# 128 rows of the last head's output weights on three DMA engines, placed between the V groups of the load stream

## The chip, the cores and the metric

One core of a Trainium2 chip runs one step of attention with a KV cache, an MLP that gates it, and a residual. The metric is device time in microseconds (us) of one execution. "Fast" and "slow" are the labels that the measurement gives: slow is a run more than 1.5% above the fastest of the same kernel.

## The reference, cut to what matters

```python
xn = layernorm(x)                                   # x: 4 x 1 x 512
q  = (xn @ wq).reshape(4, 1, 32, 128)               # wq: 512 x 4096
o  = softmax(q @ k.T * 128**-0.5) @ v               # the last 1024 keys; 8 KV heads of 4 query heads
s  = o.reshape(4, 1, 4096) @ wo                     # wo: 4096 x 512
g  = silu(gelu(layernorm(xn) @ w1 + b1) @ w2 + b2)  # w1: 512 x 1792
return x + s * g
```

Everything is bf16, the batch is 4: 29 MB are loaded and each byte is used once.

## The kernel before: the parts that matter

The program gives every engine its own list of operations with the waits that they need. SyncE issues the large loads in one order: wq and K groups, then V groups with w1 and w2 among them, then the output weights wo. A V group takes the SBUF space of a K group. A load whose space is not free makes SyncE wait, and what stands behind it waits too: in this kernel's trace SyncE waits 21.7 + 8.7 us for TensorE, and issues no later load meanwhile.

```python
load_v(0); d_w1 = dma("sp", w1 ...); load_v(1); d_w2 = dma("sp", w2 ...)
for g in range(2, HKV):
    load_v(g)
wo_r = A_wo.rearrange("(g p i) o -> p g i o", g=HKV, i=4)   # 4 rows of each head on each partition
for n, (g0, g1, i0, i1) in enumerate(((0,2,0,4), (2,4,0,4), (4,6,0,4), (6,7,0,4),
                                      (7,8,0,3), (7,8,3,4))):
    d_wo.append(dma("sp", wo_sb[:, g0:g1, i0:i1, :] <- wo_r[:, g0:g1, i0:i1, :]))
# TensorE, from "S" on: scores, PV(0), first MLP product mlp1 (w1), PV(1), second MLP product (w2), PV(2..7)
rows = to_rows(0, HKV)          # 16 products: o of all heads to the rows that wo's partitions hold
for k in range(len(d_wo)):      # 128 products in six groups, each waits for its load
    t_w = wo(k, rows)
# then: times g, transpose, plus x, store
```

The softmax here doesn't subtract the row's maximum and nothing guards it: scores larger than these inputs give would overflow.

## Time and profile before

| kernel before | |
|---|---|
| time | 76.9 to 77.1 us in the first four runs, median 77.03 |
| span of the profiled execution | 75.3 us |
| loaded | 28.85 MB, some 428 GB/s from 52.5 to 57 us |
| third wo load landed on its last engine | 69.86 us |
| last wo load landed, first and last engine | 70.42 and 72.17 us |
| first MLP product ends | 51.70 us |

"Landed" is taken from the semaphore updates in the trace: a load to 128 partitions has 16 of them, read here as one per DMA engine (the page counts 16 engines). Two lines of TensorE's timeline show how little slack its end has (columns: start, duration, engine, source line, operation, how many; in brackets its idle time before and what ended it):

```profile
68.00 1.55 PE L507 MATMUL psM<-OW,wo_sb 128*128 128x4 bf16 x53 [0.51 <-DVE OW L493]
70.13 2.35 PE L507 MATMUL psM<-OW,wo_sb 128*128 128x4 bf16 x75 [0.58 <-issue]
```

The 128 wo products run without a visible wait but for one stop of 0.58 us that no semaphore explains. It comes 764 of TensorE's matmuls and weight loads after the last such stop before it; the earlier ones, which end at 27.95, 34.43, 40.45 and 46.84 us, are 254 apart. Inside the second line TensorE waited only 0.2 us for the fifth load.

### The profile page before, as it was taken

Reading aid. Unit: us, or ns where it says so; the run is one execution under the profiler, and the core shown is the slowest. Engines: PE = TensorE matmul, PEld = TensorE weight load, DVE = VectorE, ACT = ScalarE, POOL = GpSimd, SP = SyncE. Lnnn points to the kernel's source line nnn. Section 1 sums busy time; section 2 is a strip of 40 time slices with the busy share of each in tenths; the row PEclk is TensorE's granted clock in tenths of the full one; section 3 lists DMA queues with packets and bytes.
Section 4 is the critical chain, followed back from the end, with each engine's and each line's share of the span. In section 5 each row is a group of like instructions: output and inputs, shape, how many; then the busy total and the mean of one; then the engine's idle time right before and its main releaser. Section 6 shows DMA issues by size and latency. Waiting matters only on the chain.

```text
span 75.3 us, 2297 instructions
## 1 busy us (share of the span) xinstructions
PE 50.0 (66%) x1046; PEld 39.8 (53%) x1058; DVE 39.3 (52%) x82; ACT 9.8 (13%) x16; POOL 4.6 (6%) x14
## 2 busy tenths in 40 slices
PE   0000039993859949987997994999069879818770
PEld 0000039992359939976997860104049576518740
DVE  0778107786058967985996424001664679770010
ACT  0611000000090303111130630003300000000000
POOL 6980000000000000000000000000000000000000
PEclk9999999999999999999999999569755555555555
DMA  1899999998999999999999999999999999999600
GB/s 36 244 455 405 420 422 479 435 444 370 427 422 431 422 418 431 427 414 466 401 420 453 406 443 390 427 431 409 427 427 440 418 401 416 418 420 416 252 25 2
DMA packets 4219, 28.99 MB, mean 385 GB/s; under 512 B 493, under 2 KB 625, under 8 KB 1650
## 3 DMA queue, kind: packets, MB, share of 16 engines
q1 hardware_dynamic: 4160, 28.84, 92.2%
q8 instruction: 8, 0.13, 0.6%
q10 hardware_dynamic: 50, 0.01, 0.1%
q14 instruction: 1, 0.01, 0.0%
HBM read 28.85 MB, written 0.00 MB: 383 GB/s over the span
## 4 chain that ended last, share of the span: by engine, by line
DMA 36%; PE 35%; SPq 16%; issue 5%; DVE 4%
DMA wo_sb<-in_A_wo_dram 24%; PE psK L278 22%; SPq L475 15%; DMA kv_buf<-in_A_k_cache_dram 12%; PE psS L297 7%; PE psO L362 3%; DVE kt_buf L284 2%; DVE q_sb L368 1%; PE psK L374 1%; PE psM L507 1%; PE psK L346 1%; PE psS L538 1%; SPq L212 1%; SPq L205 0%; DVE o_bf L540 0%
## 5 line engine op out<-in xcount | busy, mean ns | idle before, releaser
L278 PE MATMUL psK<-ident,kv_buf 128*128 128x128 bf16 x256 | 21.2, 237 | 11.8 <-DMA kv_buf<-in_A_k_cache_dram 10.6
L284 DVE COPY kt_buf<-psK 128x1024 bf16<-128x1024 bf16 x32 | 21.3, 691 | 8.7 <-PE psK L278 8.6
L278 PEld LDWEIGHTS psK<-ident,kv_buf 128*128 128x128 bf16 x256 | 17.1, 108 | 11.1 <-DMA kv_buf<-in_A_k_cache_dram 10.6
L297 PE MATMUL psS<-qT,kt_buf 128*128 128x16 bf16 x256 | 10.4, 169 | 1.7 <-issue 1.1
L297 PEld LDWEIGHTS psS<-qT,kt_buf 128*128 128x128 bf16 x256 | 9.4, 96 | 3.0 <-issue 2.1
L315 PEld LDWEIGHTS psO<-P_buf,kv_buf 128*128 128x128 bf16 x256 | 7.4, 102 | 3.0 <-issue 3.0
L315 PE MATMUL psO<-P_buf,kv_buf 128*128 128x16 bf16 x256 | 8.0, 173 | 1.0 <-DVE OTb L333 0.6
L328 DVE TENSOR_REDUCE den_sb<-psS 128x16 f32<-128x512 f32 x8 | 5.5, 691 | 4.2 <-PE psO L315 4.0
L305 ACT ACTIVATE P_buf<-psS 128x512 bf16<-128x512 f32 x8 | 4.8, 597 | 17.1 <-PE psS L297 17.1
L400 PE MATMUL psK<-w_sb,yT 128*32 128x512 bf16 x16 | 4.9, 1093 | 1.3 <-issue 1.3
L507 PE MATMUL psM<-OW,wo_sb 128*128 128x4 bf16 x128 | 3.9, 166 | 1.1 <-issue 0.6
L507 PEld LDWEIGHTS psM<-OW,wo_sb 128*128 128x128 bf16 x128 | 3.6, 104 | 1.4 <-issue 1.2
L411 DVE SCALAR_TENSOR_TENSOR kt_buf<-kt_buf,psK 128x512 f32<-128x512 f32 x1 | 0.7, 686 | 6.4 <-ACT kt_buf L410 6.4
L534 DVE TENSOR_TENSOR sg_sb<-psM,g_sb 128x16 f32<-128x16 f32 x1 | 0.2, 185 | 4.7 <-PE psM L507 4.7
L400 PEld LDWEIGHTS psK<-w_sb,yT 128*32 128x32 bf16 x16 | 0.5, 114 | 3.8 <-issue 3.8
L369 ACT ACTIVATE q_sb<-psO 128x512 bf16<-128x512 f32 x1 | 0.6, 597 | 13.5 <-PE psO L362 13.5
L424 PE MATMUL psK<-ident,kt_buf 128*128 128x128 bf16 x4 | 0.6, 307 | 2.4 <-DVE kt_buf L419 2.4
L331 DVE RECIPROCAL rden<-den_sb 128x16 f32<-128x16 f32 x8 | 2.0, 253 | 0.3
L362 PE MATMUL psO<-wq_sb,xT 128*32 128x512 bf16 x32 | 1.9, 380 | 0.3 <-DVE xT L351 0.3
L246 DVE CAST P_buf<-x_bf 4x512 f32<-4x512 bf16 x1 | 0.8, 795 | 2.4 <-DMA x_bf<-in_A_x_dram 2.4
L237 POOL TENSOR_SCALAR_AFFINE_SELECT negm<-zero_bf 128x512 bf16<-128x512 bf16 x1 | 1.9, 1852 | 0.1
L321 PE MATMUL psS<-P_buf,ones_bf 128*128 128x512 bf16 x3 | 1.8, 587 | 0.0
(64 smaller groups left out, 27.4 us busy)
## 6 DMA issues: line engine op xcount, KB each, us to landing
kv_buf<-in_A_k_cache_dram SPq DMA_DIRECT2D x8, 1024.0 KB, 19.9
kv_buf<-in_A_v_cache_dram SPq DMA_DIRECT2D x8, 1024.0 KB, 22.8
wq_sb<-in_A_wq_dram SPq DMA_DIRECT2D x2, 2048.0 KB, 11.3
w_sb<-in_B_w_dram SPq DMA_DIRECT2D x2, 1792.0 KB, 27.9
wo_sb<-in_A_wo_dram SPq DMA_DIRECT2D x3, 1024.0 KB, 24.3
wo_sb<-in_A_wo_dram SPq DMA_DIRECT2D x1, 512.0 KB, 21.5
wo_sb<-in_A_wo_dram SPq DMA_DIRECT2D x1, 384.0 KB, 18.2
wo_sb<-in_A_wo_dram SPq DMA_DIRECT2D x1, 128.0 KB, 18.0
```

Of the source, the lines that this page charges most:

```text
L237: c_neg = add("gp", lambda e: e.affine_select(negm[:, :], zero_bf[:, :], [[0, 32], [1, 4], [0, 4]], ALU.is_equal, NEG, base=0, channel_mul ...
L278: last = pe.transpose(psK[n % NB][:, j * 128:(j + 1) * 128], kv_buf[:, g, u * UT + j, :], ident[:, :])
L284: cp[n] = add("dve", lambda e: e.tensor_copy(kt_buf[:, n % NKT, :], psK[n % NB][:, 0:1024]), t, sc.get(n - NKT))
L297: last = pe.matmul(psS[g % 2][:, c * 16:(c + 1) * 16], kt_buf[:, n % NKT, j * 128:(j + 1) * 128], qT[:, g * 16:(g + 1) * 16], start=False, ...
L305: ex[g] = add("act", lambda e: e.activation(P_buf[:, g, :], psS[g % 2][:, 0:512], AF.Exp, scale=SCALE), sc[n])
L315: last = pe.matmul(pso[:, 0:16], kv_buf[:, (HKV + g) % NS, c, :], P_buf[:, g, c * 16:(c + 1) * 16], start=(c == 0), stop=(c == NC - 1))
L328: v = add("dve", lambda e: e.tensor_reduce(den_sb[:, cs], bass.AP(psS[g % 2], 0, [[512, 128], [1, 16], [16, NC]]), AX.X, ALU.add), den[g])
L331: v = add("dve", lambda e: e.reciprocal(rden[:, cs], den_sb[:, cs]), v)
L362: last = pe.matmul(psO[m // 4][32 * s:32 * s + 32, 0:512], xT[:, c, :], wq_sb[:, c, m * 512:(m + 1) * 512], start=(c == 0), stop=(c == 3), ...
L400: pe.matmul(psK[0][32 * s:32 * s + 32, 0:1024].bitcast(F32), yT[:, c, :], bass.AP(w1_sb, c * F + K0[s], [[4 * F, 128], [1, 4], [FC, 128]]) ...
L475: e.dma_start(wo_sb[:, g0:g1, i0:i1, :], wo_r[:, g0:g1, i0:i1, :]))))
L507: last = pe.matmul(psM[:, PS_W + c * 4:PS_W + (c + 1) * 4], wo_sb[:, g, i, c * 128:(c + 1) * 128], OW[:, i, g * 4:(g + 1) * 4], start=firs ...
```

## The change

The intent: some DMA engines finish 1.4 us before the others (the prediction says why), so give the early ones more to do and the late ones less. The last 128 rows of wo go to a space of 24 partitions, 120 of them by a load whose shape is to confine it to three engines, and stand among the V groups. The space is that of w1, so the load waits until the first MLP product has read w1.

```diff
+    wox_sb = w1_sb[0:24, ...]                       # 24 partitions x 6 rows, over w1
+    sel3, selx, OW3, OWx ...                        # selectors for the new places of the rows; 3 GpSimd selects
-        t = add("pe", fn, v_xyT, d_w1, ...)
+        t = mlp["w1"] = add("pe", fn, v_xyT, d_w1, ...)
-    for g in range(2, HKV):
-        load_v(g)
     for g in range(HKV):
+        if g >= 2:
+            load_v(g)
+        if g == 4:
+            d_wox = [dma("sp", wox_sb[:, 0:5] <- [[5*D, 3], [15*D, 8], [1, 5*D]], mlp["w1"]),  # 120 rows
+                     dma("sp", wox_sb[0:8, 5] <- [[D, 8], [1, D]], mlp["w1"])]                 # 8 rows
         PV(g)
...
-    (7, 8, 0, 3), (7, 8, 3, 4)                      # last head: 3 + 1 rows a partition
+    (p i) o, i = 3: (0, 2), (2, 3)                  # last head's first 384 rows: 2 + 1 rows a partition
-    to_rows: 16 products; wo: 128 products
+    to_rows: 16 + 9 + 6 products; wo: 112 + 24 + 12; the 24 follow the third wo load's
```

More of the change, by code (lines that the diff above doesn't have):

```diff
@@ L124, in bass_recurrent_scan__sliding_block_cached__mixer_channel_mlp__decode_kernel @@
     w2_sb = sb([128, FC, D], BF16)
+    wox_sb = w1_sb[0:24, :, :].rearrange("p c f -> p (c f)")[:, 0:6 * D].rearrange(
+        "p (j o) -> p j o", j=6)
     kt_buf = sb([128, NKT, UT * 128], BF16)
@@ L161, in bass_recurrent_scan__sliding_block_cached__mixer_channel_mlp__decode_kernel @@
     OW = sb([128, 4, HKV * 4], BF16)
+    sel3 = sb([128, 3, 3, 128], BF16)
+    selx = sb([128, 6, 24], BF16)
+    OW3 = sb([128, 12], BF16)
+    OWx = sb([24, 24], BF16)
     hT = sb([128, 64], BF16)
@@ L243, in bass_recurrent_scan__sliding_block_cached__mixer_channel_mlp__decode_kernel @@
         base=0, channel_multiplier=-1), c_o32)
+    ones_w = bass.AP(ones_bf, 0, [[128, 128], [0, 9], [1, 128]])
+    c_sel3 = add("gp", lambda e: e.affine_select(
+        sel3[:, :, :, :], ones_w, [[-128, 3], [1, 3], [3, 128]], ALU.is_equal, 0.0,
+        base=0, channel_multiplier=-1), c_1)
+    c_sx = add("gp", lambda e: e.affine_select(
+        selx[:, 0:5, :], ones_bf[:, 0:120], [[1, 5], [5, 3], [15, 8]], ALU.is_equal, 0.0,
+        base=0, channel_multiplier=-1), c_1)
+    c_sx5 = add("gp", lambda e: e.affine_select(
+        selx[:, 5, :], ones_bf[:, 0:24], [[1, 24]], ALU.is_equal, 0.0,
+        base=120, channel_multiplier=-1), c_1)
     v = add("dve", lambda e: e.tensor_copy(x32[:, :], x_bf[:, :]), d_x)
@@ L408, in fn @@
             return last
-        t = add("pe", fn, v_xyT, d_w1, d_b1, *[cp[n] for n in range(NUN - NB, NUN)])
+        t = mlp["w1"] = add("pe", fn, v_xyT, d_w1, d_b1, *[cp[n] for n in range(NUN - NB, NUN)])
         a = add("act", lambda e: e.activation(f32k(0), h_ps, AF.Square), t)
@@ L466, in bass_recurrent_scan__sliding_block_cached__mixer_channel_mlp__decode_kernel @@
         w2_sb[:, :, :], B_w2.rearrange("(p c) o -> p c o", c=FC)))
-    for g in range(2, HKV):
-        load_v(g)
-    wo_r = A_wo.rearrange("(g p i) o -> p g i o", g=HKV, i=4)
-    d_wo = []
-    for n, (g0, g1, i0, i1) in enumerate(((0, 2, 0, 4), (2, 4, 0, 4), (4, 6, 0, 4), (6, 7, 0, 4),
-                                          (7, 8, 0, 3), (7, 8, 3, 4))):
-        d_wo.append((g0, g1, i0, i1, pg.dma("sp", "wo%d" % n, lambda e, g0=g0, g1=g1, i0=i0, i1=i1:
-                                            e.dma_start(wo_sb[:, g0:g1, i0:i1, :],
-                                                        wo_r[:, g0:g1, i0:i1, :]))))
@@ L478, in to_rows @@
-    def to_rows(g0, g1):
-        psx = psS[0]
-        def fn(pe):
-            last = None
-            for i in range(4):
-                for j in range(4):
-                    last = pe.matmul(psx[32 * j:32 * j + 32, i * 32 + g0 * 4:i * 32 + g1 * 4],
-                                     sel[:, i, :],
-                                     bass.AP(OTb, g0 * 16 + j * 4,
-                                             [[HKV * 16, 128], [16, g1 - g0], [1, 4]]),
-                                     start=True, stop=True)
-            return last
-        t = add("pe", fn, ep[g1 - 1], c_sel, ex[HKV - 2])
-        return add("dve", lambda e: e.tensor_copy(
-            OW[:, :, g0 * 4:g1 * 4],
-            psx[:, 0:128].rearrange("p (i n) -> p i n", i=4)[:, :, g0 * 4:g1 * 4]), t)
@@ L497, in bass_recurrent_scan__sliding_block_cached__mixer_channel_mlp__decode_kernel @@
-    first = [True]
-    def wo(k, rows):
-        g0, g1, i0, i1, d = d_wo[k]
-        def fn(pe):
-            last = None
-            for g in range(g0, g1):
-                for i in range(i0, i1):
-                    for c in range(4):
-                        last = pe.matmul(psM[:, PS_W + c * 4:PS_W + (c + 1) * 4],
-                                         wo_sb[:, g, i, c * 128:(c + 1) * 128],
-                                         OW[:, i, g * 4:(g + 1) * 4],
-                                         start=first[0], stop=(k == len(d_wo) - 1 and i == i1 - 1),
-                                         skip_group_check=True)
-                        first[0] = False
-            return last
-        return add("pe", fn, d, rows, mlp["g"])
@@ L516, in bass_recurrent_scan__sliding_block_cached__mixer_channel_mlp__decode_kernel @@
-    for g in range(HKV):
+    for g in range(HKV):
+        if g >= 2:
+            load_v(g)
+        if g == 4:
+            R3 = (7 * 512 + 384) * D
+            d_wox = [pg.dma("sp", "wox0", lambda e: e.dma_start(
+                wox_sb[:, 0:5, :].rearrange("p j o -> p (j o)"),
+                bass.AP(A_wo.tensor, R3, [[5 * D, 3], [15 * D, 8], [1, 5 * D]])), mlp["w1"]),
+                pg.dma("sp", "wox1", lambda e: e.dma_start(
+                    wox_sb[0:8, 5, :], bass.AP(A_wo.tensor, R3 + 120 * D, [[D, 8], [1, D]])), mlp["w1"])]
@@ L528, in bass_recurrent_scan__sliding_block_cached__mixer_channel_mlp__decode_kernel, with load_wo @@
     epilogue(HKV - 1)
-    rows = to_rows(0, HKV)
-    for k in range(len(d_wo)):
-        t_w = wo(k, rows)
+    wo_r = A_wo.rearrange("(g p i) o -> p g i o", g=HKV, i=4)
+    d_wo = []
+    def load_wo(n, g0, g1, i0, i1):
+        d_wo.append((g0, g1, i0, i1, pg.dma("sp", "wo%d" % n, lambda e: e.dma_start(
+            wo_sb[:, g0:g1, i0:i1, :], wo_r[:, g0:g1, i0:i1, :]))))
+    for n, g0 in enumerate((0, 2, 4)):
+        load_wo(n, g0, g0 + 2, 0, 4)
+    load_wo(3, 6, 7, 0, 4)
+    w3_r = A_wo[7 * 512:7 * 512 + 384, :].rearrange("(p i) o -> p i o", i=3)
@@ new lines, in bass_recurrent_scan__sliding_block_cached__mixer_channel_mlp__decode_kernel, with to_rows, fn @@
+    d_w3 = [(i0, i1, pg.dma("sp", "w3%d" % i0, lambda e, i0=i0, i1=i1: e.dma_start(
+        wo_sb[:, 7, i0:i1, :], w3_r[:, i0:i1, :]))) for i0, i1 in ((0, 2), (2, 3))]
+    def to_rows():
+        psx = psS[0]
+        def fn(pe):
+            last = None
+            for i in range(4):
+                for j in range(4):
+                    last = pe.matmul(psx[32 * j:32 * j + 32, i * 28:(i + 1) * 28],
+                                     sel[:, i, :],
+                                     bass.AP(OTb, j * 4, [[HKV * 16, 128], [16, 7], [1, 4]]),
+                                     start=True, stop=True)
+            o = 7 * 16
+            for i in range(3):
+                for j in range(3):
+                    last = pe.matmul(psx[:, 128 + i * 4:132 + i * 4], sel3[:, j, i, :],
+                                     OTb[:, o + j * 4:o + j * 4 + 4],
+                                     start=(j == 0), stop=(j == 2))
+            for a in range(6):
+                last = pe.matmul(psx[0:24, 160 + a * 4:164 + a * 4], selx[:, a, :],
+                                 OTb[:, o + 12:o + 16], start=True, stop=True)
+            return last
+        t = add("pe", fn, ep[HKV - 1], c_sel, c_sel3, c_sx, c_sx5, ex[HKV - 2])
+        return [add("dve", lambda e: e.tensor_copy(
+            OW[:, :, 0:28], psx[:, 0:112].rearrange("p (i n) -> p i n", i=4)), t),
+            add("dve", lambda e: e.tensor_copy(OW3[:, :], psx[:, 128:140]), t),
+            add("dve", lambda e: e.tensor_copy(OWx[:, :], psx[0:24, 160:184]), t)]
@@ new lines, in wo, with fn @@
+    def wo(tiles, *deps):
+        def fn(pe):
+            last = None
+            for w, o, st, sp in tiles:
+                for c in range(4):
+                    last = pe.matmul(psM[:, PS_W + c * 4:PS_W + (c + 1) * 4],
+                                     w[:, c * 128:(c + 1) * 128], o,
+                                     start=(st and c == 0), stop=sp, skip_group_check=True)
+            return last
+        return add("pe", fn, *deps)
+    rows = to_rows()
+    for n, (g0, g1, i0, i1, d) in enumerate(d_wo):
+        wo([(wo_sb[:, g, i, :], OW[:, i, g * 4:(g + 1) * 4], n == 0 and g == 0 and i == 0, False)
+            for g in range(g0, g1) for i in range(i0, i1)], d, rows[0], mlp["g"])
+        if n == 2:
+            wo([(wox_sb[:, a, :], OWx[:, a * 4:(a + 1) * 4], False, False) for a in range(5)]
+               + [(wox_sb[0:8, 5, :], OWx[0:8, 20:24], False, False)], rows[2], *d_wox)
@@ L534, in bass_recurrent_scan__sliding_block_cached__mixer_channel_mlp__decode_kernel @@
+    for i0, i1, d in d_w3:
+        t_w = wo([(wo_sb[:, 7, i, :], OW3[:, i * 4:(i + 1) * 4], False, i == 2)
+                  for i in range(i0, i1)], d, rows[1])
     v = add("dve", lambda e: e.tensor_tensor(
```

## The prediction

A second path in (d), about 74.3, lay below the 74.8 that went into the sum.

> **What bounds the kernel now.** I read the page first (slices, chain of waits), then the chain in order of time, the SyncE timeline (who issues loads, when), the TensorE timeline around the MLP, and last the landings that the trace records for each load, one per DMA engine.
>
> ```profile
> span 75.3 us, 2297 instructions
> ...
> PEclk9999999999999999999999999569755555555555
> DMA  1899999998999999999999999999999999999600
> ...
> DMA 36%; PE 35%; SPq 16%; issue 5%; DVE 4%
> ```
>
> The 16 DMA engines are at 90% or more from the second slice to about 71 us, and TensorE runs at half clock in the tail. 28.85 MB at some 420 GB/s is 69 us: the kernel is a load stream, and it is fast only as long as that stream has no hole.
>
> ```profile
> 41.68 0.37 SPq L205
> 42.04 0.04 issue
> 42.09 0.59 SPq L475
> ...
> 53.69 18.16 DMA wo_sb<-in_A_wo_dram
> 71.86 0.05 issue
> 71.90 0.60 PE psM L507 x16
> ```
>
> The end hangs on the output-weight (wo) loads: 18.2 us from issue to landing, so a load waits some 18 us behind earlier ones. That backlog is the kernel's cushion.
>
> ```profile
> 71.00:72.00 1.00, 0.94 (x35) 0.86 (x33) 0.00 (x0) 0.00 (x0) 0.00 (x0) 0.50 0.35 124
> ```
>
> From 71 us only a third of the DMA time is used. The landing records say why: the last load ends at 70.42 to 70.73 on eight engines, at 71.37 to 72.17 on the other eight. Each 16 KB packet of TensorE's instruction queue (starting 25.5, 32.2, 38.3, 44.5, 50.5, 60.6, 67.8 us), or the one 8 KB instruction packet at 41.2, adds one engine to the late group: it loses about 1.2 us (0.7 for the small one). This skew is what the change is after.
>
> ```profile
> 28.74 0.53 SPq L205 DMA_DIRECT2D kv_buf<-in_A_v_cache_dram  x1
> 31.55 0.54 SPq L205 DMA_DIRECT2D kv_buf<-in_A_v_cache_dram  x1
> ...
> 50.63 1.07 PE L404 MATMUL psK<-b_sb,ones_bf 1*32 1x512 bf16 x4
> 51.64 0.97 PE L315 MATMUL psO<-P_buf,kv_buf 128*128 128x16 bf16 x32
> ...
> 51.76 0.60 ACT L410 ACTIVATE kt_buf<-psK 128x512 f32<-128x512 f32 x1 [7.43 <-PE psK L404]
> ```
>
> These lines decide the case. SyncE issues V group 3 at 28.74 and V group 4 at 31.55, long before they move. The first MLP product (L400, then its bias at L404) ends at 51.70, when ScalarE takes it.
>
> [...]an 8-row load of x has nine semaphore updates[...], a 4-row load five, a one-row load two.
> [...]SyncE's waits for TensorE come to 21.7 + 8.7 us, and no later load of that queue is issued in them.
> [...]Here the first load is issued at 0.80 to 1.19 and its first packet starts at 1.83 (1.03 us after the issue began); the store is issued at 73.49 and its first packet starts at 74.35 (0.86). I use the trace's 0.9 to 1.0.
> [...]packets of 16384 bytes, and stalls of TensorE every 254 instructions or so (26.9, 33.6, 40.0, 69.4 us).
>
> **The change part by part.**
> (a) Bytes. The last 128 of the 4096 wo rows leave the 16-engine loads: 8 KB less on each engine, at 306 ns for 8192 bytes: 0.31 us less. Three engines get 8 packets of 5120 bytes instead (40 KB, 1.53 us), eight get 1 KB more (0.04). Had this stood in the stream without a wait, undisturbed engines would have had 1.4 us of slack for a net 1.2 us, and the stream would have ended about 0.3 us earlier.
> (b) The wait. The rows go into the space of w1, so the load waits for the first MLP product, and it stands in SyncE's queue between V groups 3 and 4. Listing the built program shows it: the load waits for TensorE's semaphore, the three V loads behind it wait for nothing more. SyncE, which issued V group 4 at 31.55, now sleeps until 51.72. All that is queued then ends with V group 3, whose landing before was 50.62 on undisturbed engines and 52.54 on the last. So the cushion is eaten up.
> (c) The restart. Wake 51.72; two issues at 0.36 each (as the 16-row store took) plus 0.05 between; V group 4 is issued from 52.5, and its first packets start 0.9 to 1.0 later, at 53.5. The first packets after an empty queue are slow (1.03 to 1.47 us for 16 KB at the start, 0.61 later), so 0.3 more. An undisturbed engine idles 50.3 to 53.5, a late one 52.2 to 53.5.
> (d) The rest of the stream. An undisturbed engine took 70.42 - 50.62 = 19.8 us from the landing of V group 3 to its last; less 0.31 it is 19.5. With 0.3 from last byte to recorded landing: 53.5 + 0.3 + 19.5 + 0.3 = 73.6. The hole realigns the engines, so the old skew is gone, but instruction packets at 60.6 and 67.8 us follow and each puts 1.2 us on one engine: 74.8. [...]The last landing goes from 72.17 to 74.8: **+2.6 us**.
> (e) TensorE's tail. 31 instead of 16 products turn OTb into rows, and 148 instead of 128 multiply wo, at 26.7 ns apart: 20 x 0.027 = 0.53, and 15 x 0.02 = 0.3 plus two small VectorE copies. Alone, with the fetch stall at 69.4 (over at 70.13), the tail would have 110 products left where it had 74: 0.9 us more, less the 0.2 it waited at 71.7; +0.7. But with the late stream it sits in the wait for wo, except that about 84 products remain when the third wo load lands (about 72.7): 2.2 us, 74.9. So both finish together; I add nothing beyond 0.1.
> (f) Three more GpSimd selects: 1152, 120 and 24 elements a partition against 1.85 us for 512; about 4.7 us after 5.5 us, done by about 11, needed at 67. Nothing.
> Sum: +2.6 -0.1 for the roundings, 76.99 + 2.5 = **79.5 us**, 3.3% slower.
>
> **The rivals.**
> 1. The intended gain: [...]the others end 0.31 us earlier: 76.7. For it: the skew of 1.4 us is real. Against: it needs the load to be issued while there is a backlog, and the wait forbids that; also TensorE's tail (e) would then take over.
> 2. TensorE's tail is the bound: 76.99 + 0.7 = 77.7, "same". For it: TensorE was busy with only 0.2 us of waiting from 70.13 to the end. It holds if the hole is much smaller than I think, say because the queue holds more at 51.7 than V group 3. The landing records speak against that: loads complete in the order of issue.
> 3. The hole costs more: issuing to an empty queue takes longer, V groups land later than their products want them, and the chain of V products and reciprocals (1.4 us a group) shifts. V group 7 would land at 64 to 65.2, where its product started at 64.45, so this begins to bind: up to 0.8 later, mostly hidden behind wo. [...]Then 80.3.
>
> **Range and chances.** The main term is the restart time, good to half a microsecond; the instruction packets and the three engines are good to 0.7. So 78.8 to 80.3 eight times in ten. The line of 2% is 78.53, 1.0 below my number; only rival 2 or half a hole gets there. Slower 0.90, same 0.09, faster 0.01.
>
> **What would show it right or wrong.** In the new trace: SyncE's timeline with a wait of about 19 us for the product of psK and V group 4 issued near 52.5; a dip in the DMA row and in GB/s at 51 to 53.5 us; V group 4 landing at 56 to 57.5 instead of 54.8; the last wo landing near 74.8[...]. If V group 4 is issued before 40 us, or the DMA row shows no dip, step (b) is wrong and rival 1 or 2 holds. If the dip is there but the end moves by under 1.5 us, the stream had slack that I did not see. The tail is right if TensorE's last products begin within 0.1 us of the last landing.

## The result, and the profile after

The four runs that came with the result are 78.31, 79.34, 78.02 and 79.33 us: median 78.82, against 77.03 before. The two above 79 us are slow, the other two fast. The ratio of the fast runs is **1.015** (95% interval 1.011 to 1.0189), "same" by the 2% rule and slower beyond doubt. A ratio is the mean time of one kernel's fast runs over that of the other's of the same rounds, so not quite the ratio of the medians. The prediction said 79.5, at least 78.8, and slower by over 2%. That the median of the four touches its range is luck: two of them happened to be slow.

The page of the profiled execution (a fast run, 78.31 us):

```profile
span 76.6 us, 2387 instructions
...
PE 49%; DMA 35%; SPq 5%; DVE 5%; issue 4%
```

SyncE's timeline and ScalarE's first MLP operation, to set beside the same lines of before:

```profile
49.56 0.87 SPq L492 DMA_DIRECT2D w_sb<-in_A_wo_dram  x1
49.57 0.60 ACT L429 ACTIVATE kt_buf<-psK 128x512 f32<-128x512 f32 x1 [7.14 <-PE psK L423]
50.48 0.40 SPq L495 DMA_DIRECT2D w_sb<-in_A_wo_dram  x1
50.93 1.87 SPq L212 DMA_DIRECT2D kv_buf<-in_A_v_cache_dram  x3
```

The wait is there: SyncE sleeps until the first MLP product ends. But it ends at 49.5, not 51.7, and the three V loads behind it are groups 5, 6 and 7, not 4 to 7. V group 5 is issued at 50.93, before group 4 has landed (53.07 to 55.54). So the queue has not run dry. The stretches of one microsecond after that, before and after (columns: stretch, length, busy time of PE, PEld, DVE, ACT, POOL, then granted clock, DMA share, GB/s):

```profile
53.00:54.00 1.00, 0.00 (x0) 0.00 (x0) 0.30 (x2) 0.63 (x1) 0.00 (x0) 0.80 1.03 434
54.00:55.00 1.00, 0.03 (x1) 0.03 (x2) 0.88 (x2) 0.00 (x0) 0.00 (x0) 0.50 1.05 442
55.00:56.00 1.00, 0.71 (x6) 0.43 (x6) 0.38 (x2) 0.00 (x0) 0.00 (x0) 0.50 1.01 426
```

```profile
53.00:54.00 1.00, 0.71 (x18) 0.47 (x16) 0.73 (x2) 0.00 (x0) 0.00 (x0) 0.50 0.97 341
54.00:55.00 1.00, 1.00 (x44) 1.00 (x42) 0.51 (x3) 0.00 (x0) 0.00 (x0) 0.50 1.02 311
55.00:56.00 1.00, 1.00 (x43) 1.00 (x41) 0.35 (x2) 0.18 (x1) 0.00 (x0) 0.50 0.97 329
```

The DMA share stays at 0.97 to 1.02, so every engine is busy, yet the bytes fall by a quarter. A busy engine is not a fast one. Before, every packet of 8192 bytes that starts from 52.5 to 57 us takes 309 to 313 ns; here 53 of 178 take over 330 ns, 27 of them 500 to 1512. Below, such a stretch, in which the engines are busy and the bytes fall, is called a dip, and one in which engines are idle a hole. Measured against 428 GB/s from 52.5 to 57 us, 329 KB are missing (3 KB before). The stretch begins with the first 5120-byte packet of the new load (53.0 us) and outlives the last of these (55.0 us) by some 0.7 us (360 GB/s from 55.5 to 55.75, 426 in the quarter after).

The chain of waits ends so:

```profile
54.22 16.96 DMA wo_sb<-in_A_wo_dram
71.18 0.05 issue
71.22 2.60 PE psM L560 x84
```

The third wo load lands at 71.18 instead of 69.86, and 84 products follow it. Before, 64 followed, and the last of those waited for the last loads. TensorE's last product ends at 73.82 instead of 72.5; that is the +1.3 us of this execution.

### The profile page after: what moved, and what is told of

Read it like the earlier page. It is cut to its first block, busy times and chain, and to the rows that moved or that the text cites. A ratio compares the mean times of both kernels' runs of the same rounds, so it can differ in the third digit from the quotient of the medians.

```text
span 76.6 us, 2387 instructions
## 1 busy us (share of the span) xinstructions
PE 52.2 (68%) x1093; PEld 40.4 (53%) x1093; DVE 39.4 (51%) x84; ACT 9.8 (13%) x16; POOL 6.5 (8%) x17
## 4 chain that ended last, share of the span: by engine, by line
PE 49%; DMA 35%; SPq 5%; DVE 5%; issue 4%
DMA wo_sb<-in_A_wo_dram 22%; PE psK L297 21%; DMA kv_buf<-in_A_k_cache_dram 12%; PE psS L316 8%; PE psK L419 6%; PE psM L560 3%; DVE kt_buf L303 3%; PE psO L381 3%; PE psS L312 3%; SPq L212 2%; PE psO L334 2%; SPq L515 2%; PE psK L423 1%; DVE q_sb L387 1%; PE psK L393 1%
## 5 line engine op out<-in xcount | busy, mean ns | idle before, releaser
L297 PE MATMUL psK<-ident,kv_buf 128*128 128x128 bf16 x256 | 20.7, 235 | 11.6 <-DMA kv_buf<-in_A_k_cache_dram 10.8
L340 PE MATMUL psS<-P_buf,ones_bf 128*128 128x512 bf16 x8 | 4.3, 534 | 0.0
L312 PE MATMUL psS<-negm,ind 128*128 128x512 bf16 x8 | 3.0, 380 | 0.0
```

Source lines behind the costliest of these rows:

```text
L297: last = pe.transpose(psK[n % NB][:, j * 128:(j + 1) * 128], kv_buf[:, g, u * UT + j, :], ident[:, :])
L312: pe.matmul(psS[g % 2][:, 0:512], ind[:, :], negm[:, :], start=True, stop=False, skip_group_check=True)
L340: den[g] = add("pe", lambda pe: pe.matmul(psS[g % 2][:, 0:512], ones_bf[:, :], P_buf[:, g, :], start=True, stop=True), ex[HKV - 2 + g % 2] ...
```

## The experiments

Three theories: **W**, the wait (loads issued late or in a burst); **P**, the place: it matters which partitions the new load writes; **H**, three engines reading one stretch of HBM. The author chose the partitions for P by an assumption on which of them each engine writes in a load to 128. The traces carry no engine numbers, so it was not shown. What the runs can answer is whether the partitions matter. The changed kernel writes the 120 rows to partitions 0 to 23, below the *joined* partitions; the versions for P write them to 0 to 11 and 32 to 43, the *split* partitions. Where a label or a text says "own", the split partitions are meant; "foreign" means others, here 12 to 23 or the joined ones.

All runs were correct, beside 7 to 11 runs of the kernel before at 76.8 to 77.5 us. "KB missing" is as above, from the packets in the trace of one run.

| run | edit | times, us | ratio of fast runs | KB missing |
|---|---|---|---|---|
| e0_after | control | 77.65 to 79.52 | 1.0116 | 791 (a slow run) |
| e2_wait_only | wait, nothing else | 77.01 to 78.14 | 1.006 | 7 (a fast run) |
| e1_early | no wait | 77.61 to 77.84 | 1.0083 | 249 |
| e3_own_ports | wait, split partitions, two loads (13 updates each) | 78.18 to 78.92 | 1.0189 | 509 |
| f1_early_ports | no wait, split partitions | 76.98 to 77.22 | 1.0013 | 6 |
| g3_half_foreign | no wait, joined partitions, two loads | 77.44 to 77.89 | 1.0061 | 238 |
| f3_wait_ports | wait, split partitions | 77.42; 79.34 to 79.84 | none | 951 (a slow run) |
| g2_wait_later | wait, split partitions, after V7 | 76.88 to 77.36; 78.04 to 78.09 | 1.0002 | see there |
| f4_early_first | no wait, its products first | 77.46 to 78.0 | 1.0093 | 232 |
| f2_early_ports_first | no wait, split partitions, products first | 76.79 to 77.03 | 0.9992 | 6 |
| g1_four_engines | no wait, partitions 0 to 15, products first, meant for 4 engines | 77.09 to 77.94 | 1.0028 | 3 |

### The changed kernel again (e0_after)

No edit.

> The changed kernel again, as a control. In its first trace no DMA engine is ever idle, but the stream's rate falls from 428 GB/s to 338, 318 and 307 GB/s in the three microseconds from 53 to 56 us, from the packet where the load on three engines starts. All theories expect the same dip of about 320 KB again and a time of 78.0 to 79.4 us. If the dip is missing in this trace while the time stays, the dip is not the cause.

Times 79.52, 77.65, 78.29, 79.23: with the first four, a fast group of 77.65 to 78.31 (mean 78.07) and a slow one of 79.23 to 79.52 (mean 79.36). The granted clocks overlap (0.822 to 0.836 and 0.794 to 0.824), so the clock doesn't part the groups. The profiled run was a slow one, and its trace is another case than the one of the fast run:

```profile
51.98 0.60 ACT L429 ACTIVATE kt_buf<-psK 128x512 f32<-128x512 f32 x1 [7.38 <-PE psK L423]
53.33 1.87 SPq L212 DMA_DIRECT2D kv_buf<-in_A_v_cache_dram  x3
```

And its stretches of one microsecond:

```profile
53.00:54.00 1.00, 0.00 (x0) 0.00 (x0) 0.30 (x2) 0.63 (x1) 0.00 (x0) 0.87 0.52 174
54.00:55.00 1.00, 0.00 (x0) 0.00 (x0) 0.96 (x2) 0.00 (x0) 0.00 (x0) 0.50 0.86 193
```

Here the MLP product ends at 51.97 and V group 5 is issued at 53.33, when group 4 has landed on eight of the sixteen engines. The DMA share falls to 0.52: engines are idle. This is the hole that the prediction described, one V group further on. The last wo load lands at 74.46. Most of the 2.4 us by which the MLP product ends later goes to stops of TensorE that no semaphore explains, some 254 of its instructions, or a multiple, apart: from 25 to 47 us two of them, 1.6 us in all, in the fast run, and four, 3.6 us, in the slow one. The 16 KB packets of the instruction queue (q8 of the page) are read as TensorE's, since each of TensorE's five stops of over 0.4 us that no semaphore explains in the kernel before begins 1.2 to 1.8 us after one of them starts. They start at 22.2, 29.4 and 36.2 us in the fast run, at 25.7, 32.2 and 38.2 in the slow one (25.5, 32.2 and 38.3 in the kernel before). Why they come early or late was not found. The kernel before does not care; with the wait, SyncE does.

### The wait alone (e2_wait_only)

```diff
-        cache_rows(A_v_cache, g)), t_last[...] ...)
+        cache_rows(A_v_cache, g)), t_last[...] ..., mlp["w1"] if g == 5 else None)   # in the kernel before
```

> The kernel before with the wait alone: V group 5 is issued only after the first MLP product, no row goes elsewhere, products as before. Theory W (the wait: loads issued late and in a burst slow the engines) expects the dip after the restart and +0.8 to +1.3 us, about 78.1. Theory P[...] and theory H (three engines reading the same stretch of HBM) expect no dip as long as V group 5 is issued before V group 4 has landed, and 77.0 to 77.4 us.

77.09, 77.92, 78.14, 77.01 us. In the profiled run (77.09) the MLP product ends at 49.8, V group 5 is issued then, well before group 4 lands, the rate stays above 400 GB/s (7 KB missing) and the last landing is 72.25 us, as before:

```profile
54.00:55.00 1.00, 1.00 (x37) 0.98 (x38) 0.90 (x3) 0.00 (x0) 0.00 (x0) 0.50 1.01 426
```

So in this run a wait and a burst of issues cost nothing and make no dip: the dip is not W's. The two slower runs, 0.9 to 1.1 us above the kernel before, are not explained. A late MLP product is one guess, but with its end at 51.7, as in the kernel before, V group 5 would by estimate still be issued 1.4 us before group 4 begins to land (53.08). No trace of one was caught.

### The load without the wait (e1_early)

```diff
-    wox_sb = w1_sb[0:24, ...]
+    wox_sb = wq_sb[0:24, ...]          # free since about 20 us
-    ..., mlp["w1"])
+    ..., t_q)                          # the product that reads wq; long done
```

The space of wq serves instead of that of w1.

> The changed kernel with the rows put into the space of wq, free since 20 us, so that the load is issued without a wait at about 33 us, at the same place in the stream. Theory W expects the dip to vanish, the last wo landing near 71.9 us and a time of 76.7 to 77.5 (TensorE's longer tail takes part of it). Theories P and H expect the same dip of about 320 KB around 53 to 56 us and 78.0 to 78.8 us as in the changed kernel.

77.61 to 77.84 us, all in one group. SyncE issues the load at 31.01, with no wait, and the stream still falls:

```profile
54.00:55.00 1.00, 0.71 (x11) 0.43 (x10) 0.54 (x2) 0.00 (x0) 0.00 (x0) 0.50 1.19 333
55.00:56.00 1.00, 1.00 (x44) 1.00 (x41) 0.70 (x3) 0.00 (x0) 0.00 (x0) 0.50 0.84 296
```

W falls as the reason of this dip: the load itself makes it. The scatter mostly goes with the wait, though.

### The split partitions, first try (e3_own_ports)

```diff
-    wox_sb[:, 0:5] <- [[5*D, 3], [15*D, 8], [1, 5*D]]
+    wox_sb[32*h:32*h+12, 0:5] <- [[20*D, 3], [5*D, 4], [1, 5*D]]   for h in 0, 1
```

> The changed kernel, wait and all, but the 120 rows go in two loads of 12 partitions each, to partitions 0 to 11 and 32 to 43[...]. Theory P expects the dip to go (rate above 410 GB/s from 53 to 56 us) and 76.9 to 77.6 us. Theory H and theory W expect the dip to stay and 78.0 to 78.8 us.

It tested something else. The semaphores of the two loads have 13 updates each instead of 4: by the reading above twelve engines. The author's guess at the reason is that the source's steps of 20 rows and of 5 rows make one series of 12; the pattern of the next version, of which that can't be said, has 4. It is slower than the changed kernel's fast runs (1.0189), its MLP product ended late (51.65), and hole and dip overlap (509 KB). It says nothing on P against H. Count the updates of a semaphore before believing how many engines a load uses.

### The split partitions (f1_early_ports)

```diff
+    wox_sb[32*h:32*h+12, 0:5] <- [[5*D, 3], [15*D, 4], [1, 5*D]]   for h in 0, 1     # no single series
     (and no wait, as in the early load)
```

> The early load (no wait), and this time really on three engines[...]: two loads of 12 partitions, to 0-11 and 32-43, with a source pattern that does not merge. Theory P[...] expects the dip of the early load (310 and 314 GB/s between 54 and 56 us) to vanish, the last wo landing near 71.9 us and 77.0 to 77.4 us, against 77.7 of the early load. Theory H (three engines reading one stretch of HBM) expects the same dip and 77.6 to 77.8 us.

Four updates a load, read as three engines. The dip is gone (6 KB missing) and so is the cost, 77.10 against 77.71 us:

```profile
54.00:55.00 1.00, 1.00 (x43) 1.00 (x41) 0.07 (x1) 0.17 (x1) 0.00 (x0) 0.50 0.99 415
55.00:56.00 1.00, 1.00 (x29) 0.72 (x26) 0.35 (x2) 0.01 (x1) 0.00 (x0) 0.50 1.03 434
```

The same rows, the same bytes, three engines: H falls. (The 8-row load, to partitions 0 to 7, is unchanged here and makes no dip that can be seen.) The last landing is 72.28, not 71.9: fifteen of the sixteen updates have come by 71.94, the last 0.34 later. Its engine the trace doesn't name; the guess is one that has both the extra rows and an instruction packet.

### The joined partitions in two loads (g3_half_foreign)

```diff
-    wox_sb[32*h:32*h+12, 0:5]     # 0-11 and 32-43
+    wox_sb[12*h:12*h+12, 0:5]     # 0-11 and 12-23; the source as it was
```

> The early load in two loads of 12 partitions as in the version with own partitions, same source rows and order, but the second goes to partitions 12 to 23 instead of 32 to 43[...]. Theory P expects about half of the dip or more (loss of 110 KB or more between 53 and 57 us) and 77.3 to 77.6 us. If splitting in two or the order of rows took the dip away, there is none and 77.1 us.

The dip is back, 238 KB, at 77.55 us:

```profile
54.00:55.00 1.00, 0.31 (x4) 0.32 (x4) 0.63 (x1) 0.00 (x0) 0.00 (x0) 0.50 1.24 314
```

Only the destination partitions of the second load differ from the version without a dip (12 to 23 instead of 32 to 43), so neither two loads nor the order of rows took it away: P stands, in that the partitions decide. But half of the 120 KB goes where it made no dip, and the loss is still nearly that of the early load (249 KB), so it is not in proportion to the bytes that go elsewhere. Why the partitions matter, and how they slow the packets of the other loads, is open. Over all traces in which the queue did not run dry, the four with the joined partitions (changed kernel, e1, g3, f4) miss 232 to 329 KB; of the versions with the load in the same position, the two with the split ones (f1, f2) miss 6 KB and the one with partitions 0 to 15 (g1) 3 KB. The dip is clear; what it costs in time is less so. The profiled run is the slowest of the six (77.89): its MLP product ends late (51.47), and TensorE runs the wo products with no wait for a load, so the end is TensorE's there. The other five are 77.44 to 77.6, without a trace.

### The split partitions with the wait (f3_wait_ports)

```diff
     wox_sb over w1_sb, mlp["w1"] kept; partitions and source as in f1
```

> The changed kernel with the wait[...]. If the costs of the wait and of the foreign partitions add up, this has the wait's cost alone (0 to 1.1 us with the moment at which the first MLP product ends, as in the kernel with the wait alone): 77.0 to 78.2 us. Theory H expects 77.7 to 79.4 us, as the changed kernel.

79.84, 79.36, 77.42, 79.34 us. The one fast run is within the expectation (77.42, cheaper than every fast run of the changed kernel), the slow ones are worse than it said, and no faster than those of the changed kernel. In the trace of a slow one the MLP product ends at 51.68 and the three small loads keep SyncE busy until V group 5 is issued at 53.87; the DMA share falls to 0.29 in the microsecond from 54. Splitting the load has lengthened the hole: V group 5 comes 0.54 us later than in the slow run above. So what the joined partitions add in the slow runs is not shown.

### The wait after V group 7 (g2_wait_later, h_late_a, h_late_b, h_late_c)

```diff
-        if g == 4:  d_wox = [...]       # between V groups 4 and 5
+    d_wox = [...]                       # after V group 7, ahead of wo; partitions and wait as in f3
```

> Own partitions and the full wait for the first MLP product (the rows go into w1's space), but the load stands after V group 7 instead of between groups 4 and 5, so that three more V groups (7.3 us) are queued while SyncE waits. If the wait costs only because the queue runs dry, it costs nothing here: 77.0 to 77.3 us in every run, no run above 77.5, no fall of the rate below 395 GB/s from 52 to 66 us. If a wait in SyncE's queue costs by itself, the times scatter from 77.4 to 79.8 as with the wait at the early place.

This missed: 76.88, 77.36, 78.06, 78.09, 76.88, 78.04. So a queue that runs dry is not all there is to the scatter.

> The kernel with the wait after V group 7 once more, a single look, to catch one of its slow runs (78.05 us, half of six). If the slow runs are the ones in which the first MLP product ends late (near 51.7 us) and the queue still runs dry, the rate falls below 300 GB/s in some microsecond after the V groups. If the stream stays full, the last landing stays near 72 us and TensorE's late chain makes the end: products of wo start after 68 us and run without a wait to the end.

> As the look before it: a second chance to catch a slow run of the wait after V group 7.

> As the look before it: a third chance to catch a slow run of the wait after V group 7.

They came out at 77.94, 76.91 and 77.92 us. In the first the MLP product ends at 51.73, yet the stream is full (418 GB/s or more from 52 to 57 us; from 59.5 to 64 us, where the new load passes, 408 to 418 in the four traces of this version and 412 in the kernel before) and the last wo load lands at 71.89 us, before that of the kernel before. The end is TensorE's:

```profile
68.58 1.15 PE psM L562 x38
69.73 0.36 issue
70.09 3.37 PE psM L562 x110
73.46 0.02 issue
```

The wo products start at 68.58, and the 148 of them run to 73.46 with no wait for a load (the kernel before: 68.00 to 72.5). The third look is like the first: 51.72, then 68.57 to 73.43. In the fast look the MLP product ends at 50.62, the wo products start at 67.48, 1.1 us earlier, and run as closely. So here a late TensorE costs 1.0 us by its longer tail: the 15 more products of the turn to rows and the 20 more of wo. The prediction had put this at 0.7. The fast look also serves against the early load: in that one's trace TensorE is as late (50.60, wo products from 67.36), but with the dip the last load lands at 72.78 instead of 71.93, and the run took 77.70 instead of 76.91 us. Beside the partitions, the position of the load in the queue differs in this pair.

### The tail's order (f4_early_first), everything together (f2_early_ports_first), four engines (g1_four_engines)

```diff
-    wo loads 0, 1, 2, then the 24 products, then the rest
+    the 24 products first, then wo loads 0, 1, 2 and the rest        # f4 on e1, f2 on f1
+    g1: one load, wox_sb[0:16, 0:8] <- [[8*D, 4], [32*D, 4], [1, 8*D]]; meant for four engines, 8 rows a partition
```

> The early load, whose 24 products now come before those of the first wo load, while TensorE would wait for the third wo load anyway. If the 20 added products cost time at the end (84 products follow the third wo load, 2.2 us), this gives 0.2 to 0.4 us back: 77.3 to 77.5. If the last landing alone sets the end, nothing: 77.7.

77.46 to 78.0 us, median 77.71: no gain over the early load. The number is that of the expectation's second case, but not by its reason, the last landing (72.60). In its trace the MLP product ended late (51.5), and TensorE ran its wo products from 70.10 to 73.20 without a wait: moved work is no less work when TensorE has no gap to put it in.

> Everything together: early, own partitions, products first. With theory P and the tail's cost this is the intended gain: last landing near 71.9 us and 76.6 to 77.0 us, at best 0.3 us under the kernel before. Theory H expects 77.3 to 77.5 us.

76.79 to 77.03 us, ratio 0.9992 (interval 0.9979 to 1.0006). All the harm is gone, and no gain is to be seen. Its last landing is 72.22 us.

> A try for a better version: one load on four engines to 16 partitions of 8 rows each[...], early, its 32 products first. 32 KB on each of four engines instead of 40 on three. I expect the last landing at 71.7 to 72.3 us and 76.7 to 77.1 us: under the kernel before by at most 0.3 us.

Six runs of 77.09 to 77.94, ratio 1.0028. No dip (3 KB), last landing 72.24 us. No version beats the kernel before.

### One more look at the wait alone (h_wait_a)

No edit.

> The kernel before with the wait alone, a single look, to catch one of its slow runs (77.9 to 78.1 us). If the slow run is the one with the late MLP product, V group 5 is issued near 51.7 us and the rate falls below 350 GB/s between 52 and 55 us.

77.01 us: a fast one, with the MLP product at 50.07 and no dip. The slow case of the wait alone stays unseen in a trace.

## Why the prediction was wrong, point by point

- **The step that failed is (b).** It said of the load: "it stands in SyncE's queue between V groups 3 and 4". It stands between 4 and 5, as the change above has it; the prediction's own "three V loads behind it" can only be groups 5 to 7, so the listing was misread. V group 4 was issued at 30.27 us, which the prediction had named as a sign that (b) is wrong. All that follows in (c) and (d), an idle stretch from 50.3 to 53.5 and V group 4 landing at 56 to 57.5, was a V group (2.4 us) too pessimistic. V group 4 landed at 53.07 to 55.54, beside 53.06 to 54.82 before.
- **(b) also took 51.72 as given** for the end of the MLP product, from one trace. It is 49.5 in the trace of the fast run and 51.97 in that of the slow one, where group 5, not 4, was late. In the fast run there is no hole at all: the largest term of the sum was zero.
- **In its place: the destination partitions.** No step had this. Without the wait and with the tail as it was, moving the load from the joined to the split partitions took the time from 77.71 to 77.10 us: 0.6 of the 1.0 us that the fast runs of the changed kernel lost (249 KB at 428 GB/s are also 0.6 us). The prediction counted 1.53 us for three engines and nothing for the other thirteen.
- **(c)** took 0.36 us for each small issue. They took 0.87 and 0.40 (a V group's issue took 0.53 to 0.54 before). **(d)** took 1.2 us for an instruction packet; by the landings before, the seven latest engines end 1.4 us after the eight earliest (means 72.00 and 70.57).
- **(a)**: the last landing with the load early and on the split partitions was 72.2 to 72.3, not 71.9. With the load after V group 7 it was 71.89 to 71.96 in three traces and 72.18 in a fourth, beside 72.17 before: there the stream did end up to 0.3 us earlier, but no version was clearly faster.
- **(e) and rival 2** were closer than the weight they got: 1.0 us where 0.7 was reckoned, in the run in which nothing else was wrong and TensorE was late. (f) had no part that shows.
- **The slow runs**, 79.2 to 79.5, look like a hit for 79.5. They are luck: the hole came a V group later than predicted, and the load that makes a dip in the fast run was in it too. How the 791 KB of that trace divide between hole and dip is not shown, so the last landing of 74.46 beside a predicted 74.8 confirms no term.
- **Rival 1**, the intended gain, was rightly set aside, though its reason (no backlog) held only in the slow runs.
- **Open**: why the instruction packets come early or late; how the partitions that one load writes slow the packets of the others; the remaining 0.4 us of the fast runs (78.07 beside 77.71 for the early load). A smaller hole is not needed for it: the one fast run with a trace (78.31) has none, yet it misses 80 KB more than the early load and its last load lands at 73.41 instead of 72.78. The wait may have a part in this, as the two slower runs of the wait alone are unexplained.

## What to carry to other kernels

Where a load is confined to few engines, try it on other partitions: here half of it, moved from partitions 12 to 23 to partitions 32 to 43, took away a dip of 238 KB. Read the GB/s beside the DMA share, since slow packets count as busy (a share of 0.97 to 1.02 at 311 to 341 GB/s here). A wait in the queue that issues loads holds up all the loads behind it (V group 5 was issued at 50.93 and 53.33 us with it, at 33.94 without), so give the load a space that has long been free. And read a position in a queue off the listing twice, with the number of loads before and behind it: the largest term of a sum may hang on it.
